# Gelu of two feature tiles in a gated attention and MLP kernel: by five instructions on two engines, or by one ScalarE activation each

## The chip, the cores and the metric

The kernel runs on one core of a Trainium2 chip. A core has five engines that each work through a queue of their own in order: TensorE (PE, matrix products into PSUM), VectorE (DVE), ScalarE (ACT, activation functions), GpSimd (POOL) and SyncE (SP, which here issues the DMA transfers). They wait for one another by semaphores. PSUM has eight banks of 128 partitions by 512 floats. The metric is the time of one execution on the device, in microseconds (us).

## The reference

Two branches are computed from one input `x` (2048 tokens by 448 features) and mixed by a gate per token:

```python
g = sigmoid((x * gate_w).sum(-1))          # one gate per token
a = A_ref(x, wq, wk, wv, wo, beta)         # 16 heads of 28, 4 segments of 512 tokens:
                                           # causal softmax attention in a segment, plus a memory
                                           # of the earlier segments with phi(t) = t+1 if t>0 else exp(t)
# B_ref: an MLP over the tokens
h = layernorm(x)
u = einsum('bsd,sf->bdf', h, w1) + b1      # 2048 tokens -> 1792 features, for each of 448 columns
u = gelu(u, approximate=True)              # 0.5 u (1 + tanh(sqrt(2/pi) (u + 0.044715 u^3)))
y = einsum('bdf,fs->bds', u, w2) + b2      # 1792 features -> 2048 tokens
return g * a + (1 - g) * y.transpose
```

All inputs and the output are bf16.

## The kernel before

**Tiling.** Tokens are cut into 16 tiles of 128 and four chunks (segments) of 512; heads into four groups of four. The 1792 features of the MLP are 14 tiles of 128, counted by `ft` from 0 to 13.

**The MLP.** `mm1(ft)` (L1025) makes one feature tile: 16 matmuls `u{ft}-0` to `u{ft}-15`, one for each token tile, accumulate 128 features by 448 columns in one PSUM bank. Then follow five instructions (L1035 to L1048):

- `gsq` on ScalarE: Square with scale sqrt(0.044715) and bias, from PSUM to `gg`;
- `gvh` on ScalarE or VectorE: half of u plus bias, from PSUM to `vh`;
- `garg` on VectorE: (gg + 1) vh;
- `gth` on ScalarE: Tanh of it;
- `gelu` on VectorE: (gg + 1) vh into `uT[ft]`, in bf16.

The bank is free when `gsq` and `gvh` have read it. `mm2(T)` (L1052) makes a token tile `y` of the second product from all 14 `uT` tiles; its first matmul waits for all of them. `fin` (L1063) adds the attention's part, and a transfer writes the tile out.

**The attention.** `scores(p, f)` (L912) makes the instructions `sc{p}_{f}`: scores of four heads into the four PSUM banks 0 to 3 at once. `exp{p}_{f}` on ScalarE (L933) reads all four (2048 elements a partition) and writes to a slot of SBUF; the next `sc` can only write once this `exp` has read. `mask` on GpSimd (L936) follows, then `pv` (L960) and, for the memory part, `mem` on TensorE (L947), and a chain on VectorE (L974 to L997). `wo` (L1008) is the output projection, `ag` (L1017) its gating.

**The projections.** `pair` (L664) makes two products together, for q, k or v of a chunk: `lo` (for example `lok3_0`) starts the accumulation of both products in two banks, each on half of the array's rows; `prk3_0` and the like finish them. `cpk`, `cpq` and `cpv` (L701, L759, L783) copy the results out of PSUM, on ScalarE (a Copy activation) or VectorE. `ek` and `eq` (L744, L768) are the Exp of phi.

**What sets the order.** Nothing is decided while the kernel runs. `ORDER` (L286) lists by name what each engine does, in order, as a planner left it. `name@banks` says which of the PSUM banks 4 to 7 (for an `exp`, which slot) the instruction takes: `lok3_0@54` accumulates its two products in banks 5 and 4. `u12-0@7*5` is `u12-0` to `u12-4`, beginning in bank 7. `Sched.plan` (L157) gives an instruction that takes a bank a dependence on everything that used the bank's last content, and `finalize` (L212) turns dependences into semaphore waits. Every matmul is issued through `mm` (L261), so most matmuls carry the line L264 in the profile.

Around the change ScalarE's order is: `exp4_1`, `gsq13`, `eq2_2`, `gvh13`, `exp4_2`, `gsq12`, `gth13`, `cpk3_0`, `exp4_3`, `cpk3_2`, `cpk3_3`, `gth12`, `exp4_4`, `ag4`, `ag5`, `exp5_0`. TensorE's is: `sc4_2`, `u12-5` to `u12-15`, `lok3_0`, `prk3_0`, `sc4_3`, `prk3_1`, `lok3_2`, `prk3_2`, `prx3_3`, `loq3_0`, `sc4_4`, `prq3_0`, `pv8`, `wo4`, `wo5`, `sc5_0`, and later `y0`. Tile 13 is made before tile 12: `u13` is in bank 6, `u12` in bank 7.

An activation function is read from a table that ScalarE has loaded; the compiler puts an `ACT_TABLE_LOAD` in front of an activation whose function the loaded table lacks. The kernel before has one, at its start.

Of the kernel before, what the change touches and what calls it, by code (L numbers as in the profile page):

```python
# [5 lines left out]
ACT = mybir.ActivationFunctionType  # L6
# [6 lines left out]
D = 448  # L13
# [61 lines left out]
class Sched:  # L75
# [13 lines left out]
    def op(self, eng, fn, reads=(), writes=(), name=None, dma=False, out=False, cost=100.0, prio=0.0, mode="f",  # L89
           nbytes=0, rel=0.0, port=False, take=None, use=(), alt=None, space=None,  # L90
           hold=HOLD):

        o = Op()
        o.eng, o.fn, o.name, o.idx = eng, fn, name, len(self.ops)
        o.is_event, o.ev_val, o.knowledge, o.waits = False, None, None, None
        o.cost = cost
        o.lat = LAT[eng]
        o.hold = hold  # L100
        o.prio = (prio, o.idx)
        o.mode = mode
        o.tile = mode if mode in "rh" else "f"
        o.cols = False
        o.nbytes = nbytes
        o.rel = rel
        o.port = port
        o.take = take if isinstance(take, list) else [take] if take is not None else []
        o.free = use
        for g in use:  # L110
            g.left += 1
        o.alts = {eng: (fn, cost, port)}
        if alt is not None:
            o.alts[alt[0]] = (alt[1], alt[2], False)
            o.eng = None
        o.start = o.end = o.pos = None
        o.evspace = eng if alt is None else None
        if dma:
            self._dma_uid += 1
            o.evspace = space or "dma_u%d" % self._dma_uid  # L120
            o.is_event = True
        if out:
            self.out_spaces.add(o.evspace)
        deps, order = {}, {}

        def need(d):
            if d is not o:
                deps[d.idx] = d

        def after(d):  # L130
            if d is not o:
                order[d.idx] = d

        for r in reads:
            if r.last_write is not None:
                need(r.last_write)
            if r.psum and eng != "PE":
                for rd in r.reads:
                    if rd.eng != "PE" and (rd.eng != o.eng or o.eng is None):
                        need(rd)  # L140
        for r in writes:
            w = r.last_write
            if w is not None:
                (after if r.psum and eng == "PE" and w.evspace == "PE" else need)(w)
            for rd in r.reads:
                (after if r.psum and eng == "PE" and rd.evspace == "PE" else need)(rd)
        o.deps = list(deps.values())
        o.order = list(order.values())
        for r in reads:
            r.reads.append(o)  # L150
        for r in writes:
            r.last_write = o
            r.reads = []
        self.ops.append(o)
        return o
# [112 lines left out]
def pe_cost(*cols):  # L268
    return sum(max(c, 64) / 2.4 + 2.0 for c in cols)


def act_cost(n, sbuf=False, ptr=0):
    return n / 1.2 + (95.0 if sbuf else 50.0) + 92.0 * ptr
# [6 lines left out]
def pool_cost(n):  # L280
    return n / 1.2 + 180.0
# [12 lines left out]
u7-11*5 loq2_0@57 prq2_0 prq2_1 u9-0@6 sc2_2 u9-1*3 loq2_2@57 prq2_2h mem4@4 u9-4*5 sc2_3 u9-9*7 prq2_2 pv4@4 sc2_4  # L294
wo1@5 wo0#1@6 wo2@4 sc3_0 wo3@7 lot8@64 prt8 prt9 mem5@7 sc3_1 pv5@7 u10-0@6*6 sc3_2 lot10@57 prt10 prt11 mem6@4
u10-6*5 sc3_3 mst1@5 u10-11*5 u11-0@4*2 pv6@5 sc3_4 u11-2*14 u13-0@6 sc4_0 u13-1*7 mem7@5 pv7@4 u13-8 sc4_1 u13-9*7
u12-0@7*5 sc4_2 u12-5*11 lok3_0@54 prk3_0 sc4_3 prk3_1 lok3_2@67 prk3_2 prx3_3 loq3_0@54 sc4_4 prq3_0 pv8@6 wo4@7
wo5@5 sc5_0 wo6@6 wo7@7 pv9@5 mem9@6 prq3_1 sc5_1 y0-0@7*13 sc5_2 y0-13 y2-0@5*4 mem8@4 y2-4*5 sc5_3 y2-9*5 mem10@6
y1-0@7*2 pv10@4 sc5_4 y1-2*11 sc6_0 y1-13 y4-0@5*10 sc6_1 y4-10*4 y5-0@7*7 sc6_2 mem11@4 pv11@5 y5-7*4 lot14@64
prt14 sc6_3 y5-11*3 y3-0@5*9 sc6_4 mst2@7 y3-9*4 loq3_2@67 prq3_2h prq3_2 y3-13 prt15 y6-0@6*2 sc7_0 lot12@57 prt12  # L300
prt13 y6-2*5 sc7_1 y6-7 pv12@4 pv13@5 wo8@7 mem12@4 y6-8*3 wo10@5 wo11@7 mem14@4 y6-11 y11-0@5*4 mem13@7 sc7_2
# [7 lines left out]
exp1_0@5 gth1 gth0 exp1_1@6 gsq2 gvh2 gsq3 gth2 gth3 gsq4 gvh4 ek1_0 gth4 ek0_3 eq1_3 exp1_2@2 gsq6 gvh6 exp1_3@3  # L309
gth6 gsq5 exp1_4@0 ek1_1 gth5 exp2_0@1 gsq8 ek1_2 gvh8 exp2_1@4 gsq7 gth8 exp2_2@5 gth7 ek1_3 exp2_3@6 gsq9 cpq2_2  # L310
exp2_4@0 gth9 ag0 ag2 exp3_0@2 cpv8 cpv9 gt8 exp3_1@3 gt9 eq2_1 ek2_0 exp3_2@1 cpv11 gt10 ek2_1 exp3_3@4 gsq10
eq2_3 gvh10 exp3_4@0 gth10 gsq11 exp4_0@5 gt11 eq2_0 gth11 exp4_1@6 gsq13 eq2_2 gvh13 exp4_2@7 gsq12 gth13 cpk3_0
exp4_3@2 cpk3_2 cpk3_3 gth12 exp4_4@3 ag4 ag5 exp5_0@0 ek2_2 eq3_0 cpq3_1 exp5_1@1 eq3_1 exp5_2@4 exp5_3@5 ek2_3
exp5_4@6 exp6_0@2 exp6_1@3 exp6_2@7 cpv14 exp6_3@0 gt14 exp6_4@1 cpq3_2 cpq3_2#1 cpv15 eq3_2 gt15 exp7_0@4 cpv12
gt12 gt13 exp7_1@5 ag8 ag10 ag11 eq3_3 exp7_2@6 exp7_3@2 exp7_4@3 ag9 ag12 ag13 ag14 ag15""",
    "DVE": """
# [7 lines left out]
msta0 mk1_1 mstc0 mstc0#1 mstc0#2 mstc0#3 gelu5 ta3 phk1_1 mk1_2 garg8 phk1_2 cpq2_0 cpq2_1 gvh7 gelu8 garg7 rec3  # L324
tm4 gelu7 oa3 eps4 mk1_3 ot3 gvh9 ta4 garg9 rec4 cpq2_2#1 oa4 gelu9 ag3 om4 phk1_3 tm5 ag1 eps5 ta5 ot4 rec5 mq2_1
cpv10 oa5 phq2_1 tm6 om5 msta1 eps6 mk2_0 mstc1 ta6 mstc1#1 mstc1#2 mstc1#3 garg10 rec6 ot5 om6 gvh11 gelu10 garg11
tm7 oa6 gelu11 eps7 ta7 phk2_0 rec7 ot6 garg13 om7 oa7 gvh12 gelu13 cpk3_1 garg12 ot7 cpq3_3 cpq3_0 gelu12 ta8
gcol2 mq2_2 omg2 mq2_3 ag6 b2g2 ag7 ta9 phq2_3 mk2_2 mk2_1 phk2_2 phk2_1 mq2_0 tm9 phq2_0 fin0 eps9 tm8 rec9 eps8
phq2_2 rec8 oa9 oa8 fin2 om9 mk2_3 om8 fin1 ot9 phk2_3 ta10 fin4 ot8 tm10 tm11 eps10 ta11 eps11 rec10 rec11 oa10
om10 fin5 oa11 msta2 ot10 mstc2 mstc2#1 mstc2#2 fin3 mstc2#3 om11 mq3_0 mq3_2 cpv13 ot11 gcol3 phq3_0 ta12 omg3  # L330
# [25 lines left out]
def build_kernel(nc, X, WQ, WK, WV, WO, BETA, W1, B1, W2, B2, GW, OUT):  # L356
    NSL, NP = 3, 5
    sch = Sched(nc, {"psum": (4, 5, 6, 7), "p": tuple(range(NP))}, {"p": (NP, NP + 1, NP + 2)})
    op = sch.op
# [10 lines left out]
    def sb(shape, dt=BF16):  # L370
        return hold(nc.sbuf_tensor(shape, dt))
# [9 lines left out]
    def bank(b):  # L381
        return ps[:, b.bank if isinstance(b, Bank) else b, :]

    def bres(b):
        return b.res if isinstance(b, Bank) else R_bank[b]
# [4 lines left out]
    def buse(b):  # L390
        return {"use": (b,)} if isinstance(b, Bank) else {}
# [17 lines left out]
    uT = sb([128, NFT, D])  # L409
# [12 lines left out]
    b1c = sb([128, NFT], F32)  # L422
# [54 lines left out]
    R_uT = R("uT", NFT)  # L477
# [6 lines left out]
    R_ident, R_bst, R_beta, R_bias, R_b2g = R("ident"), R("bst", 2), R("beta"), R("bias"), R("b2g")  # L484
# [35 lines left out]
    for st, rs, name in ((gstage, R_gst, "g"), (bstage, R_bst, "b")):  # L520
        op("POOL", lambda e, st=st: e.memset(st[:].bitcast(U32), 0), writes=rs, name="sz" + name, cost=100, prio=-5.0)
    op("SP", lambda e: e.dma_start(gstage[0:3, :], GW[0:384].rearrange("(c p) -> c p", p=128)),
       writes=[R_gst[0]], name="ldgw", dma=True, prio=-3, cost=500, nbytes=2000)
    op("SP", lambda e: e.dma_start(gstage[3:4, :], GW[320:448].rearrange("(c p) -> c p", p=128)),
       writes=[R_gst[1]], name="ldgwb", dma=True, prio=-3, cost=500, nbytes=2000)
# [5 lines left out]
       name="ldbeta", dma=True, prio=-3, cost=500, nbytes=8000)  # L531
    op("SP", lambda e: e.dma_start(bstage[0:NFT, :], B1.rearrange("(t p) -> t p", p=128)), writes=[R_bst[0]],
       name="ldb1", dma=True, prio=-3, cost=500, nbytes=8000)
    op("SP", lambda e: e.dma_start(bstage[NFT : NFT + NT, :], B2.rearrange("(t p) -> t p", p=128)),
       writes=[R_bst[1]], name="ldb2", dma=True, prio=-3, cost=500, nbytes=8000)
# [5 lines left out]
    def ring_load():  # L541
# [15 lines left out]
    P_BASE, P_ATT, P_PROJ, P_WO, P_M1, P_M2 = 0.0, 100.0, 200.0, 300.0, 400.0, 500.0  # L557
# [9 lines left out]
       reads=[R_ident], writes=[R_ident], name="id1", cost=300)  # L567
# [8 lines left out]
    for k, ap in enumerate((kT[:, 3, :], qT[:, 3, :])):  # L576
        op("POOL", lambda e, ap=ap: e.memset(ap.bitcast(U32), 0), writes=[R_z3[k]] + (R_qT if k else R_kT)[3],
           name=f"z3_{k}", cost=pool_cost(S // 2))
    vpad = vaug.bitcast(U32).rearrange("p t (h c) -> p (t h) c", c=16)
    for k, val in enumerate((0x3F80, 0)):  # L580
        op("POOL", lambda e, k=k, val=val: e.memset(vpad[:, :, 14 + k : 15 + k], val), reads=R_v if k else [], writes=R_v,
           name=f"v{k}", cost=pool_cost(256))
# [442 lines left out]
    def mm1(ft):  # L1025
        b = Bank()
        q = ft % 2
        fb, f2 = divmod(ft, 2)
        w1c = slots[fb % NSL].rearrange("p (t f) -> p t f", t=NT)
        for st in range(NT):  # L1030
            op("PE", lambda e, cols=False, st=st: mm(e, bank(b)[:, 0:D], w1c[:, st, f2 * 128 : f2 * 128 + 128],
                                                     xh[:, st, :], cols, start=(st == 0), stop=(st == NT - 1)),
               reads=[R_slot[fb % NSL][st // 4], R_x[st]], writes=[bres(b)], take=b if st == 0 else None, name=f"u{ft}-{st}", mode="x", cost=pe_cost(448),
               prio=P_M1 + ft)
        op("ACT", lambda e: e.activation(gg[:, q, :], bank(b)[:, 0:D], ACT.Square, bias=b1s[:, ft : ft + 1],  # L1035
                                         scale=math.sqrt(GC)),
           **buse(b), reads=[bres(b), R_bias], writes=[R_gg[q]], name=f"gsq{ft}", cost=act_cost(448, ptr=1), prio=P_BASE)
        op("ACT", lambda e: e.activation(vh[:, q, :], bank(b)[:, 0:D], ACT.Identity, bias=b1h[:, ft : ft + 1],  # L1038
                                         scale=0.5),
           **buse(b), reads=[bres(b), R_bias], writes=[R_vh[q]], name=f"gvh{ft}", cost=act_cost(448, ptr=1), prio=P_BASE,  # L1040
           alt=("DVE", lambda e: e.tensor_scalar(vh[:, q, :], bank(b)[:, 0:D], 0.5, b1h[:, ft : ft + 1], op0=ALU.mult,  # L1041
                                                 op1=ALU.add), dve_cost(448)))
        op("DVE", lambda e: e.scalar_tensor_tensor(gg[:, q, :], gg[:, q, :], 1.0, vh[:, q, :], op0=ALU.add,  # L1043
                                                   op1=ALU.mult),
           reads=[R_gg[q], R_vh[q]], writes=[R_gg[q]], name=f"garg{ft}", cost=535, port=True, prio=P_BASE)
        op("ACT", lambda e: e.activation(gg[:, q, :], gg[:, q, :], ACT.Tanh, scale=2.0 * GS), reads=[R_gg[q]],  # L1046
           writes=[R_gg[q]], name=f"gth{ft}", cost=act_cost(448, True), prio=P_BASE)
        op("DVE", lambda e: e.scalar_tensor_tensor(uT[:, ft, :], gg[:, q, :], 1.0, vh[:, q, :], op0=ALU.add,  # L1048
                                                   op1=ALU.mult),
           reads=[R_gg[q], R_vh[q]], writes=[R_uT[ft]], name=f"gelu{ft}", cost=535, port=True, prio=P_BASE)  # L1050
# [143 lines left out]
```

## Time and profile before

| | |
|---|---|
| median of 3 runs | 176.94 us (176.91 to 177.38) |
| profiled execution, span from first to last instruction | 175.3 us |
| between that span and the median (what lies around it) | 1.64 us |
| TensorE (PE) busy | 169.6 us |
| VectorE (DVE) busy | 149.3 us |
| ScalarE (ACT) busy | 133.7 us |
| GpSimd (POOL) busy | 69.3 us |
| mean granted TensorE clock | 1.000 |

The page gives the span as the profiled execution's own time; the times of the runs are measured from outside it. A busy time counts the instructions of an engine from start to end, merged where they overlap. Matmuls are pipelined and their ends are modelled, so a busy TensorE is not the same as TensorE at its peak. The chain of waits follows the work that ended last back from the end: at each step to what released it. "Idle before, releaser" is the time an engine stood still ahead of an instruction, and whose semaphore ended it.

### The profile page before, as it was taken

Reading aid. Unit: us, or ns where it says so; the run is one execution under the profiler, and the core shown is the slowest. Engines: PE = TensorE matmul, PEld = TensorE weight load, DVE = VectorE, ACT = ScalarE, POOL = GpSimd, SP = SyncE. Lnnn points to the kernel's source line nnn. Section 1 sums busy time; section 2 is a strip of 40 time slices with the busy share of each in tenths; the row PEclk is TensorE's granted clock in tenths of the full one; section 3 lists DMA queues with packets and bytes.
Section 4 is the critical chain, followed back from the end, with each engine's and each line's share of the span. In section 5 each row is a group of like instructions: output and inputs, shape, how many; then the busy total and the mean of one; then the engine's idle time right before and its main releaser. Section 6 shows DMA issues by size and latency. Waiting matters only on the chain.

```text
span 175.3 us, 5601 instructions
## 1 busy us (share of the span) xinstructions
PE 169.6 (97%) x2354; PEld 82.0 (47%) x2354; DVE 149.3 (85%) x337; ACT 133.7 (76%) x170; POOL 69.3 (40%) x93
## 2 busy tenths in 40 slices
PE   8899999899999999998999999999999999999994
PEld 3443434345544544534544344444444544555653
DVE  5599999799995899998999999997889999893213
ACT  2377898999589999999999999987878977404200
POOL 8002027442302234346846644359474435550000
PEclk9999999999999999999999999999999999999999
DMA  5989973799939726942061440208567100366221
GB/s 145 295 155 290 265 148 86 176 303 228 218 105 251 210 62 184 240 105 49 0 173 41 120 130 24 60 26 243 135 193 207 51 2 4 111 184 196 69 82 52
DMA packets 50472, 24.62 MB, mean 140 GB/s; under 512 B 14976, under 2 KB 50208, under 8 KB 50448
## 3 DMA queue, kind: packets, MB, share of 16 engines
q1 hardware_dynamic: 50160, 24.05, 56.0%
q8 instruction: 18, 0.29, 0.8%
q10 hardware_dynamic: 288, 0.23, 0.4%
q14 instruction: 6, 0.05, 0.1%
HBM read 18.76 MB, written 2.36 MB: 121 GB/s over the span
## 4 chain that ended last, share of the span: by engine, by line
PE 89%; DVE 5%; DMA 3%; ACT 1%; SPq 0%; issue 0%
PE t L264 76%; PE t L924 7%; PE t L960 5%; DMA t<-in_A_wk_dram 3%; PE t L810 1%; DVE t L1048 1%; DVE t L987 0%; DVE t L883 0%; ACT t L701 0%; DVE t L703 0%; DVE t L1041 0%; ACT t L1035 0%; DVE t L1021 0%; DVE t L974 0%; DVE t L976 0%
## 5 line engine op out<-in xcount | busy, mean ns | idle before, releaser
L264 PE MATMUL t<-t 128*32 128x448 bf16 (+10 forms) x1620 | 145.3, 346 | 1.9 <-DVE t L619 0.7
L264 PEld LDWEIGHTS t<-t 128*32 128x32 bf16 (+2 forms) x1620 | 66.5, 97 | 67.1 <-issue 13.3
L933 ACT ACTIVATE t<-t 128x2048 bf16<-128x2048 f32 x40 | 75.7, 1892 | 6.0 <-PE t L924 5.8
L936 POOL TENSOR_SCALAR_AFFINE_SELECT t<-t 128x512 bf16<-128x512 bf16 x64 | 46.9, 734 | 57.6 <-ACT t L933 53.8
L1063 DVE SCALAR_TENSOR_TENSOR t<-t 128x448 bf16<-128x448 f32 (+2 forms) x17 | 10.9, 652 | 12.8 <-PE t L264 12.8
L991 POOL TENSOR_TENSOR t<-t 128x448 bf16<-128x448 f32 x12 | 14.6, 1217 | 9.7 <-DVE t L989 9.1
L1017 ACT ACTIVATE t<-t 128x448 bf16<-128x448 f32 x12 | 8.5, 726 | 10.3 <-PE t L264 10.1
L924 PE MATMUL t<-t 28*128 28x512 bf16 (+3 forms) x256 | 15.8, 301 | 0.0
L876 POOL TENSOR_TENSOR t<-t 128x4 f32<-128x4 f32 x4 | 4.5, 1130 | 20.3 <-DVE t L874 20.3
L960 PE MATMUL t<-t 128*32 128x512 bf16 (+3 forms) x256 | 11.3, 299 | 0.6 <-DVE t L974 0.6
L976 DVE STREAM_TRANSPOSE t<-t 128x512 f32<-128x512 f32 x16 | 11.2, 700 | 0.8 <-PE t L960 0.8
L924 PEld LDWEIGHTS t<-t 28*128 28x128 bf16 x256 | 4.5, 92 | 13.8 <-ACT t L933 7.4
L997 DVE STREAM_TRANSPOSE t<-t 128x512 bf16<-128x512 bf16 x16 | 10.9, 687 | 0.0
L1043 DVE SCALAR_TENSOR_TENSOR t<-t 128x448 f32<-128x448 f32 x14 | 8.8, 636 | 1.5 <-ACT t L1038 1.5
L1048 DVE SCALAR_TENSOR_TENSOR t<-t 128x448 bf16<-128x448 f32 x14 | 9.8, 705 | 0.2 <-ACT t L1046 0.2
L1035 ACT ACTIVATE t<-t 128x448 f32<-128x448 f32 x14 | 9.1, 656 | 1.1 <-PE t L264 1.1
L867 DVE BATCH_NORM_STATS2 t<-t 128x6 f32<-128x448 bf16 x16 | 9.4, 607 | 0.1
L1046 ACT ACTIVATE t<-t 128x448 f32<-128x448 f32 x14 | 8.2, 598 | 1.5 <-DVE t L1043 1.5
L960 PEld LDWEIGHTS t<-t 128*32 128x32 bf16 x256 | 6.8, 97 | 5.4 <-DVE t L974 0.8
L987 DVE SCALAR_TENSOR_TENSOR t<-t 128x448 f32<-128x448 f32 x12 | 9.2, 775 | 0.1
L974 DVE STREAM_TRANSPOSE t<-t 128x512 f32<-128x512 f32 x12 | 8.4, 697 | 0.4
L989 DVE TENSOR_TENSOR t<-t 128x448 f32<-128x448 f32 x12 | 8.2, 685 | 0.0
(69 smaller groups left out, 143.5 us busy)
## 6 DMA issues: line engine op xcount, KB each, us to landing
t<-in_B_w_dram SPq DMA_DIRECT2D x52, 256.0 KB, 4.1
out_dram<-t SPq DMA_DIRECT2D x15, 112.0 KB, 1.8
t<-in_A_x_dram SPq DMA_DIRECT2D x3, 448.0 KB, 4.6
t<-in_B_w_dram SPq DMA_DIRECT2D x8, 128.0 KB, 3.8
t<-in_A_wo_dram SPq DMA_DIRECT2D x4, 98.0 KB
t<-in_A_wq_dram SPq DMA_DIRECT2D x1, 336.0 KB, 5.3
t<-in_A_wv_dram SPq DMA_DIRECT2D x1, 336.0 KB, 5.5
spare_heads<-t SPq DMA_DIRECT2D x8, 32.0 KB
```

The source lines that it names most:

```text
L264: last = e.matmul(out[q], w[:, q], x, skip_group_check=True, **kw)
L867: op("DVE", lambda e: e.bn_stats(st6[:, t, :], xh[:, t, :]), reads=[R_x[t]], writes=[R_st6[t]], name=f"bns{t}", cost=512, prio=P_PROJ - 10 ...
L924: last = e.matmul(bank(hl)[:, c0 : c0 + w], kT[r, hg, s * 512 + j * 128 : s * 512 + j * 128 + 128], qT[r, hg, s * 512 + 128 * j : s * 512 ...
L933: op("ACT", lambda e: e.activation(pslot(g), ps[:, 0:4, :], ACT.Exp, scale=SCALE), reads=R_bank[0:4], writes=[g.res], take=g, name=f"exp{p ...
L936: op("POOL", lambda e, c0=c0: e.affine_select(pslot(g)[:, :, c0 : c0 + 128], pslot(g)[:, :, c0 : c0 + 128], pattern=[[0, 4], [1, 128]], co ...
L960: last = e.matmul(bank(cb)[32 * hl : 32 * hl + 32, 128 * j : 512], vaug[:, 4 * s + j, 32 * h : 32 * h + 32], pslot(P_fill[u // 2][f])[:, h ...
L976: dv(lambda e: e.transpose(t2[:, 0, :], bank(cb)[:, 0:512]), [bres(cb)], [R_tt[tb][0]], "ta", 630, use=(cb,))
L987: dv(lambda e: e.scalar_tensor_tensor(n3[0], n3[0], oc, rb[0], op0=ALU.mult, op1=ALU.mult), [R_tt[tb][0], R_rec[tb], R_omcol], [R_tt[tb][0 ...
L991: op("POOL", lambda e: e.tensor_tensor(o3, n3[0], n3[1], op=ALU.add), reads=R_tt[tb], writes=[R_ob[tb]], name=f"o{u}", cost=1280, port=Tru ...
L997: dv(lambda e: e.transpose(oT[:, hg, s * 512 : s * 512 + 512], o), [R_ob[tb]], qres(hg, s), "ot", 635)
L1048: op("DVE", lambda e: e.scalar_tensor_tensor(uT[:, ft, :], gg[:, q, :], 1.0, vh[:, q, :], op0=ALU.add, op1=ALU.mult), reads=[R_gg[q], R_vh ...
L1063: op("DVE", lambda e: e.scalar_tensor_tensor(outst[:, p, c0:c1], bank(b)[:, 0 : c1 - c0], omg[:, T : T + 1], ag(T)[:, c0:c1], op0=ALU.mult ...
```

## The change

For tiles 12 and 13 the five instructions are replaced by one activation, `gl12` and `gl13`: ScalarE's own Gelu function in its tanh form, read from PSUM with the bias column `b1c`, written to `uT` in bf16. Its table is not the one that Exp is read from, so the table is switched ahead of them and again before the next function that it lacks. The other twelve tiles stay as they were. In `ORDER` the instructions that are gone are taken out; `gl13` and `gl12` stand one after the other between `exp4_2` and `cpk3_0`; and the banks of three later pairs and two output projections are renumbered.

```diff
 "PE"
 u12-0@7*5 sc4_2 ...
-                    u12-5*11 lok3_0@54 prk3_0 sc4_3 prk3_1 lok3_2@67 prk3_2 prx3_3 loq3_0@54 sc4_4 prq3_0 pv8@6 wo4@7
-wo5@5 sc5_0 wo6@6 wo7@7 ...
+                    u12-5*11 lok3_0@74 prk3_0 sc4_3 prk3_1 lok3_2@65 prk3_2 prx3_3 loq3_0@74 sc4_4 prq3_0 pv8@6 wo4@5
+wo5@7 sc5_0 wo6@6 wo7@7 ...
 "ACT"
-... exp4_1@6 gsq13 eq2_2 gvh13 exp4_2@7 gsq12 gth13 cpk3_0
-exp4_3@2 cpk3_2 cpk3_3 gth12 exp4_4@3 ag4 ag5 ...
+... exp4_1@6 eq2_2 exp4_2@7 gl13 gl12 cpk3_0
+exp4_3@2 cpk3_2 cpk3_3 exp4_4@3 ag4 ag5 ...
 "DVE"
-tm7 oa6 gelu11 eps7 ta7 phk2_0 rec7 ot6 garg13 om7 oa7 gvh12 gelu13 cpk3_1 garg12 ot7 cpq3_3 cpq3_0 gelu12 ta8
+tm7 oa6 gelu11 eps7 ta7 phk2_0 rec7 ot6 om7 oa7 cpk3_1 ot7 cpq3_3 cpq3_0 ta8
 def mm1(ft): ... # after the 16 matmuls
+        if ft >= 12:
+            op("ACT", lambda e: e.activation(uT[:, ft, :], bank(b)[:, 0:D], ACT.Gelu_apprx_tanh,
+                                             bias=b1c[:, ft : ft + 1], scale=1.0),
+               **buse(b), reads=[bres(b), R_bias], writes=[R_uT[ft]], name=f"gl{ft}", cost=act_cost(448, ptr=1), prio=P_BASE)
+            return
```

More of the change, by code (lines that the diff above doesn't have):

```diff
@@ L296 @@
 u10-6*5 sc3_3 mst1@5 u10-11*5 u11-0@4*2 pv6@5 sc3_4 u11-2*14 u13-0@6 sc4_0 u13-1*7 mem7@5 pv7@4 u13-8 sc4_1 u13-9*7
-u12-0@7*5 sc4_2 u12-5*11 lok3_0@54 prk3_0 sc4_3 prk3_1 lok3_2@67 prk3_2 prx3_3 loq3_0@54 sc4_4 prq3_0 pv8@6 wo4@7
-wo5@5 sc5_0 wo6@6 wo7@7 pv9@5 mem9@6 prq3_1 sc5_1 y0-0@7*13 sc5_2 y0-13 y2-0@5*4 mem8@4 y2-4*5 sc5_3 y2-9*5 mem10@6
+u12-0@7*5 sc4_2 u12-5*11 lok3_0@74 prk3_0 sc4_3 prk3_1 lok3_2@65 prk3_2 prx3_3 loq3_0@74 sc4_4 prq3_0 pv8@6 wo4@5
+wo5@7 sc5_0 wo6@6 wo7@7 pv9@5 mem9@6 prq3_1 sc5_1 y0-0@7*13 sc5_2 y0-13 y2-0@5*4 mem8@4 y2-4*5 sc5_3 y2-9*5 mem10@6
 y1-0@7*2 pv10@4 sc5_4 y1-2*11 sc6_0 y1-13 y4-0@5*10 sc6_1 y4-10*4 y5-0@7*7 sc6_2 mem11@4 pv11@5 y5-7*4 lot14@64
@@ L311 @@
 exp2_4@0 gth9 ag0 ag2 exp3_0@2 cpv8 cpv9 gt8 exp3_1@3 gt9 eq2_1 ek2_0 exp3_2@1 cpv11 gt10 ek2_1 exp3_3@4 gsq10
-eq2_3 gvh10 exp3_4@0 gth10 gsq11 exp4_0@5 gt11 eq2_0 gth11 exp4_1@6 gsq13 eq2_2 gvh13 exp4_2@7 gsq12 gth13 cpk3_0
-exp4_3@2 cpk3_2 cpk3_3 gth12 exp4_4@3 ag4 ag5 exp5_0@0 ek2_2 eq3_0 cpq3_1 exp5_1@1 eq3_1 exp5_2@4 exp5_3@5 ek2_3
+eq2_3 gvh10 exp3_4@0 gth10 gsq11 exp4_0@5 gt11 eq2_0 gth11 exp4_1@6 eq2_2 exp4_2@7 gl13 gl12 cpk3_0
+exp4_3@2 cpk3_2 cpk3_3 exp4_4@3 ag4 ag5 exp5_0@0 ek2_2 eq3_0 cpq3_1 exp5_1@1 eq3_1 exp5_2@4 exp5_3@5 ek2_3
 exp5_4@6 exp6_0@2 exp6_1@3 exp6_2@7 cpv14 exp6_3@0 gt14 exp6_4@1 cpq3_2 cpq3_2#1 cpv15 eq3_2 gt15 exp7_0@4 cpv12
```

## The prediction

> **What bounds the kernel now.** First the busy times and the chain of waits on the page of the kernel before: which engine sets the end?
>
> ```profile
> PE 169.6 (97%) x2354; PEld 82.0 (47%) x2354; DVE 149.3 (85%) x337; ACT 133.7 (76%) x170; POOL 69.3 (40%) x93
> ...
> PE 89%; DVE 5%; DMA 3%; ACT 1%; SPq 0%; issue 0%
> ```
>
> TensorE is busy 97% of the span and is 89% of the chain that ended last. An average can hide stages, so next the busy times by stretch, cut where the change lies (us; columns PE, PEld, DVE, ACT, POOL, each with its instructions, then granted clock, DMA share, GB/s).
>
> ```profile
> 95.84:99.43 3.59, 3.59 (x28) 1.42 (x28) 3.41 (x8) 3.59 (x6) 1.87 (x3) 1.00 0.19 40
> 99.43:102.56 3.13, 3.13 (x21) 1.01 (x25) 3.13 (x5) 3.13 (x5) 2.78 (x4) 1.00 0.98 276
> ...
> 111.96:152.80 40.84, 40.84 (x623) 19.88 (x627) 37.74 (x75) 31.29 (x30) 23.65 (x29) 1.00 0.39 106
> ```
>
> TensorE has no idle time from here to 152.80. Where tiles 12 and 13 get their Gelu (95 to 103 us), ScalarE is just as full, and so nearly is VectorE. Later ScalarE has slack (31.29 of 40.84). So three engines run level at the change, and behind it TensorE alone sets the pace. A full bar of TensorE is modelled, so I checked it against the chain in order of time (start, length, what):
>
> ```profile
> 78.76 0.64 DVE t L974
> ...
> 93.46 2.38 PE t L264 x12
> 95.84 0.33 PE t L924 x8
> 96.17 3.26 PE t L264 x16
> 99.43 0.33 PE t L924 x4
> 99.76 2.80 PE t L264 x13
> 102.56 0.33 PE t L924 x8
> ...
> 105.70 0.33 PE t L924 x4
> ...
> 111.96 0.33 PE t L924 x8
> 112.29 2.21 PE t L264 x11
> ...
> 117.36 2.19 PE t L264 x11
> ...
> 119.87 2.19 PE t L264 x11
> ...
> 122.39 2.19 PE t L264 x11
> ...
> 172.94 0.35 DVE t L1063
> ```
>
> Eleven matmuls of the second MLP product take 2.19 us each time, twelve of the first 2.38: 0.19 us a matmul and some 0.1 for changing the array's tiling. Pieces that equal to 0.02 us are a pace, not waits. By the kernel's order the pieces around the change are: 95.84 scores sc4_2; 96.17 the last eleven matmuls of u12 (2.19, so to 98.36), then lok3_0 and prk3_0 (1.07, to 99.43); 99.43 sc4_3; 99.76 the other third-chunk projections (2.80); 102.56 sc4_4; 105.70 sc5_0.
>
> **The change part by part.** ScalarE in the same stretch, one line an instruction (start, length):
>
> ```profile
> 93.61 1.93 ACT L933 ACTIVATE t<-t 128x2048 bf16<-128x2048 f32 x1
> 95.36 0.69 ACT L1035 ACTIVATE t<-t 128x448 f32<-128x448 f32 x1
> 95.88 0.69 ACT L768 ACTIVATE t<-t 128x512 bf16<-128x512 bf16 x1
> 96.40 0.70 ACT L1038 ACTIVATE t<-t 128x448 f32<-128x448 f32 x1
> 96.92 1.95 ACT L933 ACTIVATE t<-t 128x2048 bf16<-128x2048 f32 x1
> 98.67 0.72 ACT L1035 ACTIVATE t<-t 128x448 f32<-128x448 f32 x1
> 99.19 0.67 ACT L1046 ACTIVATE t<-t 128x448 f32<-128x448 f32 x1
> 99.66 0.69 ACT L701 ACTIVATE t<-t 128x512 bf16<-128x512 f32 x1
> 100.13 1.98 ACT L933 ACTIVATE t<-t 128x2048 bf16<-128x2048 f32 x1
> ...
> 102.84 0.60 ACT L1046 ACTIVATE t<-t 128x448 f32<-128x448 f32 x1
> 103.31 1.89 ACT L933 ACTIVATE t<-t 128x2048 bf16<-128x2048 f32 x1
> ...
> 112.34 1.88 ACT L933 ACTIVATE t<-t 128x2048 bf16<-128x2048 f32 x1 [0.28 <-PE t L924]
> ```
>
> These are exp4_1, gsq13, eq2_2, gvh13, exp4_2, gsq12, gth13, cpk3_0, exp4_3, gth12, exp4_4 and, as one that waited for TensorE, exp5_2. An activation starts before the last one ends: small ones come 0.47 to 0.52 us apart, and 1.75 us lie between the start of an exp and the next start.
>
> *Removed from ScalarE:* gsq13, gvh13, gsq12 (0.52 each by starts), gth13 and gth12 (0.47 each): 2.50 us. *Removed from VectorE:* garg and gelu twice, gvh12 once. Their rows, with those of the only table load:
>
> ```profile
> L1043 DVE SCALAR_TENSOR_TENSOR t<-t 128x448 f32<-128x448 f32 x14 | 8.8, 636 | 1.5 <-ACT t L1038 1.5
> L1048 DVE SCALAR_TENSOR_TENSOR t<-t 128x448 bf16<-128x448 f32 x14 | 9.8, 705 | 0.2 <-ACT t L1046 0.2
> L1041 DVE TENSOR_SCALAR t<-t 128x448 f32<-128x448 f32 x8 | 5.3, 679 | 0.6 <-ACT t L1035 0.4
> ```
>
> ```profile
> 1.71 1.28 ACT L661 ACT_TABLE_LOAD   x1 [1.71 <-PEq L1179]
> 4.86 0.60 ACT L661 ACTIVATE t<-t 128x512 bf16<-128x512 bf16 x1 [1.87 <-PE t L645]
> ```
>
> ```profile
> L1035 ACT ACTIVATE t<-t 128x448 f32<-128x448 f32 x14 | 9.1, 656 | 1.1 <-PE t L264 1.1
> ```
>
> VectorE sheds 2 x 0.636 + 2 x 0.705 + 0.679 = 3.36 us. I count it at no gain: the chain has no VectorE piece between those at 78.76 and 172.94 us; TensorE's own work covers it.
>
> *Added:* gl13 and gl12. No Gelu is in the trace; it has the shape, the PSUM input and the one bias column of the Square on L1035, so 0.656 us, starts 0.52 apart. And two table switches, Exp's table to Gelu's ahead of gl13 and back ahead of exp4_3. The one load shown takes 1.28 us; the next activation came 1.87 us after it, waiting for TensorE. So a switch costs between nothing (if it ran beside other work) and 1.28 + 1.87 = 3.15 us (if all of that idle time belonged to it). I take 1.28, from the end of one activation to the start of the next, because the 1.87 is put down to the transpose on L645. ScalarE thus gets 1.04 + 2.56 us for 2.50.
>
> Here a rule speaks against the change: the Trainium skill, "ScalarE: Activation LUTs", section "What ACT_TABLE_LOAD costs", adds a drain of about 1.38 us to each load, 2.66 us a switch; the sum below would be 5.8 in place of 3.1 us. "ScalarE activation tables: per-element evaluation and per-set limits", section "What a function is on this engine", has two sets one load of 1283 ns apart, which is the row's figure; no row here shows a drain.
>
> *Moved:* bank 7 is where u12 accumulates, and lok3_0, which took banks 5 and 4, now takes 7 and 4. A bank passes on when its readers are done, so TensorE's in-order queue now stands at lok3_0 until gl12 has ended; behind it stand prk3_0, sc4_3 and all else. lok3_2 gets bank 6 (gl13) and 5: free by then. The queues of SP and POOL keep their order; their transfers and masks move along with their producers. Removing garg, gelu and gvh12 moves VectorE's casts up, which nothing waits for.
>
> **The sum**, in the profiled execution's own times:
>
> 1. exp4_2 no longer stands behind gvh13. It starts as exp5_2 did, 0.05 us after its scores (111.96 + 0.33 = 112.29 against 112.34): 96.17 + 0.05 = 96.22, ending at 98.10.
> 2. Load to 99.38. gl13 from there, gl12 from 99.90 to 100.56.
> 3. lok3_0 at 100.61 in place of 98.36: **first stall, 2.25 us**.
> 4. prk3_0 ends 1.07 later, 101.68; sc4_3 ends at 102.01; the projections would end at 104.81.
> 5. cpk3_0 (ScalarE, a Copy, waiting for prk3_0) runs 101.73 to 102.42, the second load to 103.70, exp4_3 to 105.58.
> 6. sc4_4 needs the four score banks that exp4_3 reads: 105.63 in place of 104.81: **second stall, 0.82 us**. Against 102.56 before, all is 3.07 us late.
>
> Is more late, or is it won back? exp4_4 starts once exp4_3, cpk3_2 and cpk3_3 are issued (103.70 + 1.75 + 0.47 + 0.47 = 106.39) and ends at 108.28; sc5_0 comes up at 105.63 + 3.14 = 108.77 (102.56 to 105.70 before). It clears it by 0.49, as before (103.31 + 1.89 = 105.20 against 105.70). Then TensorE works with nothing idle to 152.80, so it cannot win anything back. Span 175.3 + 3.07 = 178.4; the median of the runs, 176.94, lies 1.64 above the span, so the time is 176.94 + 3.07 = **180.0 us**.
>
> **The rivals.**
>
> *A. A switch costs more than the load.* The pipeline drains before it, or refills after it. With the bound of 3.15: gl12 ends at 102.43, stall 4.12; exp4_3 ends at 109.32, sc4_4 at 109.37, 6.8 us late: 183.7. Any part of it counts twice, so half the extra gives 181.9. For it: nothing ran straight after the load shown. Against: that idle time has a cause of its own.
>
> By the Trainium skill's 2.66 us ("ScalarE: Activation LUTs", "What ACT_TABLE_LOAD costs") the same steps end 5.8 us late, an estimate of 182.8. No run here shows it yet.
>
> *B. The second load stands ahead of cpk3_0.* Then it runs 100.56 to 101.84 while TensorE does lok3_0 and prk3_0; exp4_3 starts at 102.31 and ends at 104.19, before TensorE is ready at 104.81. Only the first stall stays: 2.25, 179.2. For it: a pass could reload at once. Against: one load serves the Copies, Exps, Tanhs and Squares of the whole kernel before, so a table seems to hold such simple functions, and the Copy needs no switch.
>
> *C. The loads cost no time* (run beside an exp, or not needed). gl13 starts at 97.97, gl12 ends at 99.15, lok3_0 at 99.20: 0.84 late, and sc4_4 does not wait: 177.8. For it: the first load hid behind other waits. Against: exp4_2 uses the table that the load replaces.
>
> *D. Not slower: TensorE's modelled records hide waits for VectorE.* VectorE is busy 3.13 of 3.13 us at the change; were it the true pace of the stretch to 152.80, its 3.36 us less would meet the 3.07 us of stalls: 176.94 + 3.07 - 3.36 = 176.6. It decides once the records hide 3 us of such waits. Against: equal pieces of 2.19 us, and no VectorE piece in the chain there.
>
> **How the numbers follow.** Forecast (179.5 to 180.6) 0.62; A 0.15; B 0.08; C 0.09; D 0.06. The range 178.9 to 182.9 holds the forecast, B and most of A; it leaves out C, D and A's far end, nearly 0.2. This measurement tells 0.3% (0.53 us) from no change; the three runs shown spread as little. C is slower by more than that; D is mostly within it: faster 0.02, same 0.04, slower 0.94.
>
> **What would show it.** Two table loads near 98 and 102 us, 1.28 us long, the second behind a Copy; exp4_2 starting near 96.2; a gap on TensorE of about 2.2 us released by the line of the Gelu, and one of 0.8 released by L933; the pieces after that unchanged, 3.1 us later; VectorE some 3.4 us less busy and no faster for it. No gap ahead of lok3_0, gaps over 3 us, or shorter pieces after 106 us would make the prediction wrong.

## The result, and the profile after

The changed kernel takes 181.52 us (median of four runs, 180.95 to 181.70) against 177.06 us for the kernel before beside it. The ratio taken over all the runs is 1.0243, 95% interval 1.0218 to 1.0268 (the two medians alone give 1.0252). It is slower by 2.4%, some 4.3 us. The profiled execution spans 179.6 us against 175.3, also 4.3 us more. The forecast was 180.0, within 178.9 to 182.9.

The page of the changed kernel, busy times and the chain that ended last by engine:

```profile
PE 170.5 (95%) x2346; PEld 82.1 (46%) x2354; DVE 146.0 (81%) x332; ACT 135.4 (75%) x169; POOL 68.8 (38%) x93
...
PE 81%; DVE 8%; ACT 5%; DMA 3%; issue 1%; SPq 0%
```

VectorE sheds 3.3 us, ScalarE gains 1.7, and ScalarE's share of the chain goes from 1% to 5%. Where, its timeline shows (start, length, then the idle time and what ended it):

```profile
95.39 0.67 ACT L768 ACTIVATE t<-t 128x512 bf16<-128x512 bf16 x1
96.25 1.88 ACT L933 ACTIVATE t<-t 128x2048 bf16<-128x2048 f32 x1 [0.18 <-PE t L924]
98.14 1.28 ACT L1036 ACT_TABLE_LOAD   x1
99.44 1.16 ACT L1036 ACTIVATE t<-t 128x448 bf16<-128x448 f32 x2
102.78 0.60 ACT L701 ACTIVATE t<-t 128x512 bf16<-128x512 f32 x1 [2.18 <-PE t L264]
103.40 1.28 ACT L933 ACT_TABLE_LOAD   x1
104.69 1.88 ACT L933 ACTIVATE t<-t 128x2048 bf16<-128x2048 f32 x1
```

These are eq2_2, exp4_2, the first load, both Gelu activations, cpk3_0, the second load and exp4_3. Each load takes 1.28 us and fills the gap between its neighbours but for 0.01 to 0.02 us. The second stands behind the Copy. TensorE's timeline of the same stretch:

```profile
95.80 0.40 PE L924 MATMUL t<-t 28*128 28x256 bf16 x8
96.13 2.25 PE L264 MATMUL t<-t 128*128 128x448 bf16 x11
100.74 0.61 PE L264 MATMUL t<-t 64*128 64x512 bf16 x2 [2.36 <-ACT t L1036]
101.69 1.06 PE L264 MATMUL t<-t 128*128 128x512 bf16 x2 [0.33 <-issue]
102.68 0.61 PE L924 MATMUL t<-t 28*128 28x512 bf16 x4
103.22 3.24 PE L264 MATMUL t<-t 128*128 128x512 bf16 x13
106.62 0.40 PE L924 MATMUL t<-t 28*128 28x384 bf16 x8 [0.16 <-ACT t L933]
...
109.94 0.40 PE L924 MATMUL t<-t 28*128 28x512 bf16 x4
```

They are sc4_2, the rest of u12, lok3_0, prk3_0, sc4_3, the projections, sc4_4 and sc5_0. lok3_0 waits 2.36 us for the Gelu. But then lok3_0 and prk3_0 take 1.94 us until sc4_3 (1.07 before), and the projections 3.24 in place of 2.87 (the timeline before follows below). The granted clock fits that (busy times in short windows; the third number from the end is the clock):

```profile
100.40:100.60 0.20, 0.00 (x0) 0.00 (x0) 0.00 (x0) 0.20 (x1) 0.20 (x1) 1.00 1.14 336
100.60:100.80 0.20, 0.06 (x2) 0.09 (x2) 0.00 (x0) 0.00 (x0) 0.20 (x1) 0.51 1.14 340
...
103.80:104.00 0.20, 0.20 (x2) 0.00 (x0) 0.00 (x0) 0.20 (x1) 0.00 (x0) 0.50 0.00 0
104.00:104.20 0.20, 0.20 (x2) 0.00 (x0) 0.00 (x0) 0.20 (x1) 0.00 (x0) 0.95 0.00 0
```

After 2.2 us of idle time the clock fell to half, and stayed there for 3.4 us, to 104.0.

Executions differ by some tenths in their first microseconds (the first weight load took 4.42 us in the execution of before, up to 5.13 in others), so from here on I compare the distance from sc4_2 to sc5_0, the stretch in which the change acts. The timeline of TensorE before, sc4_2, sc4_3, the projections and sc5_0:

```profile
95.77 0.40 PE L924 MATMUL t<-t 28*128 28x256 bf16 x8
...
99.36 0.39 PE L924 MATMUL t<-t 28*128 28x512 bf16 x4
99.69 2.87 PE L264 MATMUL t<-t 128*128 128x512 bf16 x13
...
105.64 0.39 PE L924 MATMUL t<-t 28*128 28x512 bf16 x4
```

9.87 us before; 95.80 to 109.94 = 14.14 after: 4.27 us more, the whole difference of the spans.

### The profile page after: what moved, and what is told of

Its sections match the earlier page's. It is cut to its first block, busy times and chain, and to the rows that moved or that the text cites. A ratio compares the mean times of both kernels' runs of the same rounds, so it can differ in the third digit from the quotient of the medians.

```text
span 179.6 us, 5586 instructions
## 1 busy us (share of the span) xinstructions
PE 170.5 (95%) x2346; PEld 82.1 (46%) x2354; DVE 146.0 (81%) x332; ACT 135.4 (75%) x169; POOL 68.8 (38%) x93
## 3 DMA queue, kind: packets, MB, share of 16 engines
HBM read 18.76 MB, written 2.36 MB: 118 GB/s over the span
## 4 chain that ended last, share of the span: by engine, by line
PE 81%; DVE 8%; ACT 5%; DMA 3%; issue 1%; SPq 0%
PE t L264 69%; PE t L924 6%; PE t L960 4%; DMA t<-in_A_wk_dram 3%; ACT t L933 2%; DVE t L1021 1%; DVE t L748 1%; PE t L810 1%; ACT t L701 1%; ACT L933 1%; ACT L1036 1%; DVE t L773 1%; DVE t L974 1%; DVE t L976 1%; ACT t L1036 1%
## 5 line engine op out<-in xcount | busy, mean ns | idle before, releaser
L264 PE MATMUL t<-t 128*32 128x448 bf16 (+9 forms) x1612 | 145.5, 347 | 5.0 <-ACT t L1036 2.4
L987 DVE SCALAR_TENSOR_TENSOR t<-t 128x448 f32<-128x448 f32 x12 | 9.2, 774 | 0.1
L701 ACT ACTIVATE t<-t 128x512 bf16<-128x512 f32 (+1 forms) x12 | 6.0, 508 | 4.2 <-PE t L264 4.1
L1048 DVE SCALAR_TENSOR_TENSOR t<-t 128x448 f32<-128x448 f32 x12 | 7.6, 642 | 1.5 <-ACT t L1043 1.5
L748 DVE SCALAR_TENSOR_TENSOR t<-t 128x512 bf16<-128x512 bf16 x12 | 8.4, 707 | 0.0
L1051 ACT ACTIVATE t<-t 128x448 f32<-128x448 f32 x12 | 6.9, 582 | 1.8 <-DVE t L1048 1.8
```

Source lines behind the costliest of these rows:

```text
L264: last = e.matmul(out[q], w[:, q], x, skip_group_check=True, **kw)
L748: op("DVE", lambda e: e.scalar_tensor_tensor(kphi[:, p, :], ks, 0.0, kphi[:, p, :], op0=ALU.max, op1=ALU.add), reads=kres(hg, tc) + [R_kph ...
```

## The experiments

The theory after the result: three things on TensorE, in a row. It waits at lok3_0 for bank 7, that is for the Gelu behind the first load; its clock falls; and sc4_4 waits for exp4_3, which stands behind the second load. VectorE's relief gives nothing. Rivals: the loads cost the time whatever the banks; the clock is only a label; VectorE was the hidden pace.

### The banks of before

```diff
-u12-5*11 lok3_0@74 ... lok3_2@65 ... loq3_0@74 ... wo4@5 wo5@7
+u12-5*11 lok3_0@54 ... lok3_2@67 ... loq3_0@54 ... wo4@7 wo5@5
```

> The changed kernel with only the PSUM bank numbers of the kernel before (lok3_0 in 5 and 4 again, lok3_2 in 6 and 7, loq3_0 in 5 and 4, wo4 in 7, wo5 in 5). Theory: the 4.4 us are TensorE standing still at lok3_0 for bank 7 (2.37 us), then running at half the granted clock until 104 us, then waiting for exp4_3 behind the second table load. With the banks back lok3_0 runs at 98.4 without a wait; lok3_2 waits 0.3 us for gl12; sc4_4 waits for exp4_3, which ends near 104.3, so it comes 1.8 us later than before in place of 4.06; no single stall over 1.6 us, so the clock stays at 1.0: 178.9 us. Rival (the two table loads and their time on ScalarE set the loss, whatever the banks): as after, 181.5 us.

Measured: 178.90 us against 176.94 before, ratio 1.0120 (1.0095 to 1.0145). TensorE's timeline, sc4_2, sc4_4 and sc5_0:

```profile
95.60 0.40 PE L924 MATMUL t<-t 28*128 28x256 bf16 x8
...
104.13 0.40 PE L924 MATMUL t<-t 28*128 28x384 bf16 x8 [1.56 <-ACT t L933]
...
107.44 0.39 PE L924 MATMUL t<-t 28*128 28x512 bf16 x4
```

11.84 us, 1.97 more than before, and the stall is now the one for exp4_3 alone. So with the banks of before the loads cost 2 us. The renumbering of the banks is the rest of the change's loss in its profiled execution: 2.30 of 4.27 us, the fallen clock included. With the clock held, as further down, it is 1.44 of 3.41.

### No switch of the table

```diff
-e.activation(uT[:, ft, :], bank(b)[:, 0:D], ACT.Gelu_apprx_tanh,
+e.activation(uT[:, ft, :], bank(b)[:, 0:D], ACT.Tanh,
```

> The changed kernel, banks as changed, but gl12 and gl13 apply Tanh, which the loaded table serves, in place of Gelu: no table is switched, and the output is not the reference's. Theory: gl12 ends near 99.15, lok3_0 waits 0.85 us for it, nothing else waits and the clock stays at 1.0: 177.9 us. Rival (the bank order alone costs the time, the loads hardly matter): over 179.5 us.

Measured: 178.33 against 176.94, ratio 1.0078 (1.0059 to 1.0098). sc4_2, lok3_0 and sc5_0:

```profile
96.12 0.40 PE L924 MATMUL t<-t 28*128 28x256 bf16 x8
...
99.63 0.39 PE L264 MATMUL t<-t 64*128 64x512 bf16 x2 [0.93 <-ACT t L1036]
...
106.99 0.39 PE L924 MATMUL t<-t 28*128 28x512 bf16 x4
```

10.87 us, 1.00 more than before. This is what the bank costs by itself with the new order of ScalarE; 0.85 was expected. The median is 0.4 us further up than this stretch explains. In the profiled execution sc4_2 comes 0.35 us later than before (96.12 against 95.77), so that much lies ahead of the stretch; of the other executions no trace shows it.

### Both undone

```diff
-ACT.Gelu_apprx_tanh ... lok3_0@74 ... lok3_2@65 ... loq3_0@74 ... wo4@5 wo5@7
+ACT.Tanh            ... lok3_0@54 ... lok3_2@67 ... loq3_0@54 ... wo4@7 wo5@5
```

> The changed kernel without its two hurts: Tanh in place of Gelu in gl12 and gl13 (no table switch, the output is not the reference's) and the bank numbers of before. What is left of the change is 3.36 us less on VectorE and 1.46 us less on ScalarE. Theory: TensorE had no idle time to give, so the work taken away buys nothing: 177.0 us, within 0.3 us of before. Rival D of the prediction (VectorE was the hidden pace): 174 to 176 us.

Measured: 177.31 against 177.21, ratio 0.9997 (0.9971 to 1.0023). sc4_2 and sc5_0:

```profile
96.27 0.40 PE L924 MATMUL t<-t 28*128 28x256 bf16 x8
...
106.14 0.39 PE L924 MATMUL t<-t 28*128 28x512 bf16 x4
```

9.87 us, to the hundredth what it was. VectorE's and ScalarE's relief is worth nothing here, and rival D falls.

### The banks alone, in the kernel before

```diff
 # the kernel before, with its five instructions for every tile
-u12-5*11 lok3_0@54 ... lok3_2@67 ... loq3_0@54 ... wo4@7 wo5@5
+u12-5*11 lok3_0@74 ... lok3_2@65 ... loq3_0@74 ... wo4@5 wo5@7
```

> The kernel before with only the changed bank numbers: lok3_0 takes bank 7, which gsq12 and gvh12 read. No Gelu activation, no table load. Theory: lok3_0 waits for gvh12 on VectorE, which ends at 100.1, so a stall of 1.8 us; exp4_3 ends near 103.7, before TensorE is at sc4_4: 1.8 us later than before, 178.9 us if the clock stays at 1.0, about 1 us more if it falls after a stall of that length. Rival (the new banks are harmless by themselves): 177.1 us.

Measured: 179.22 against 176.94, ratio 1.0134 (1.0119 to 1.0149). sc4_2, lok3_0 and sc5_0:

```profile
96.02 0.40 PE L924 MATMUL t<-t 28*128 28x256 bf16 x8
...
100.50 0.39 PE L264 MATMUL t<-t 64*128 64x512 bf16 x2 [1.89 <-DVE t L1041]
...
107.85 0.39 PE L924 MATMUL t<-t 28*128 28x512 bf16 x4
```

11.83 us, 1.96 more: the renumbered banks alone cost as much as two table loads. After 1.89 us of idle time the mean clock was still 1.0, in each of the four executions.

### Work in the stall, to hold the clock

```diff
-u12-5*11 lok3_0@74 prk3_0 ...
+u12-5*11 fill@5 lok3_0@74 prk3_0 ...   # 9 matmuls of 128x512 into bank 5, read by nobody
```

> The changed kernel with nine matmuls of 128x512 that nobody reads put ahead of lok3_0, in bank 5, which is free then: 1.95 us of work where TensorE stood still for 2.37 us. Theory: they start at 98.36 and end near 100.3, lok3_0 still starts when gl12 has ended, near 100.7; but the granted clock stays at 1.0, so lok3_0 to sc4_4 take their old time, exp4_3 ends near 105.6 and sc4_4 comes 3.1 us later than before, as the sum of the prediction has it: 180.1 us, 1.4 us faster than without the added work. Rival (the clock is only a label of the idle time, or the loss after the stall has another cause): 181.5 us.

Measured: 180.81 against 176.94, ratio 1.0219 (1.0204 to 1.0234). sc4_2, lok3_0, sc4_4 and sc5_0:

```profile
96.08 0.40 PE L924 MATMUL t<-t 28*128 28x256 bf16 x8
...
101.02 1.15 PE L264 MATMUL t<-t 64*128 64x512 bf16 x5 [0.39 <-ACT t L1036]
...
106.04 0.40 PE L924 MATMUL t<-t 28*128 28x384 bf16 x8 [0.75 <-ACT t L933]
...
109.36 0.39 PE L924 MATMUL t<-t 28*128 28x512 bf16 x4
```

lok3_0 comes 4.94 us after sc4_2, as in the changed kernel (100.74 - 95.80): the added work delays nothing. The pieces behind it have their old length (lok3_0 and prk3_0 1.08 us until sc4_3), sc4_4 waits 0.75 us for exp4_3, and the whole is 13.28 us, 3.41 more than before. Against the 4.27 of the changed kernel the fallen clock is worth 0.86 us in its profiled execution. By the medians it is less, and there the intervals overlap: 180.81 lies halfway between the theory's 180.1 and the rival's 181.5. So the held clock is shown by the trace, and its worth in the time only roughly.

### The second load moved up

One Exp of a single column after gl12 makes the second load run there:

```diff
-gl13 gl12 cpk3_0
+gl13 gl12 xx cpk3_0     # xx: Exp of one column of b1c into a spare tile
```

> The kernel with the nine added matmuls (clock kept at 1.0) and besides an Exp of one column after gl12, so that the second table load runs at once, ahead of cpk3_0, while TensorE does lok3_0 and prk3_0. Theory: the second stall (0.75 us at sc4_4 with the added matmuls alone) goes, and with it the 0.16 us by which wo4 then waits for the copies behind exp4_3; only the stall at lok3_0 stays, 2.4 us: 179.4 us. Rival (where the load stands makes no difference): 180.8 us.

> The changed kernel with only the Exp of one column after gl12, no added matmuls. Theory: at half the clock TensorE reaches sc4_4 only 0.16 us before exp4_3 ends, so the slow clock has swallowed the second stall, and moving the load up wins only those 0.16 us and the 0.16 us at wo4: 181.1 us. Rival (the second load's place is worth the 0.82 us of the prediction here too): 180.6 us.

Measured: with the added matmuls 179.68 against 177.21, ratio 1.0130 (1.0084 to 1.0176); without them 180.05, ratio 1.0157 (1.0105 to 1.0208), its runs from 179.27 to 181.11. The first two lines are sc4_2 and sc5_0 with the added matmuls; then, without them, sc4_2, lok3_0, sc4_3, sc4_4 and sc5_0:

```profile
95.28 0.40 PE L924 MATMUL t<-t 28*128 28x256 bf16 x8
...
107.58 0.39 PE L924 MATMUL t<-t 28*128 28x512 bf16 x4
```

```profile
95.62 0.40 PE L924 MATMUL t<-t 28*128 28x256 bf16 x8
...
100.56 0.39 PE L264 MATMUL t<-t 64*128 64x512 bf16 x2 [2.36 <-ACT t L1036]
...
101.64 0.40 PE L924 MATMUL t<-t 28*128 28x512 bf16 x4
...
104.77 0.40 PE L924 MATMUL t<-t 28*128 28x384 bf16 x8
...
107.92 0.39 PE L924 MATMUL t<-t 28*128 28x512 bf16 x4
```

12.30 us in both, 2.43 more than before: the second stall is gone and only the one at lok3_0 is left. The first kernel came out as the theory said. The second did not come out as written: it supposed a slow clock, but in this execution the clock stayed at 1.0 after the very 2.36 us of idle time after which it had fallen. That makes it a control for the clock, with no work added: from lok3_0 to sc4_3 it takes 1.08 us, where the changed kernel took 1.94. Of its four executions two had a mean clock of 1.0 (179.27 and 179.57 us) and two of 0.99 (181.11 and 180.53), which is what 3.4 us at half speed would give. No trace shows the latter two, and the kernel with the added matmuls, at 1.0 in all four, itself spreads by 1.4 us; so what the earlier load is worth under a slow clock stays open.

### How often the clock falls

The changed kernel once more, and beside it one with four added matmuls in place of nine:

```diff
-        for _ in range(9):
+        for _ in range(4):
             last = e.matmul(bank(fb_), ones[:, 0:128], ones, start=True, stop=True, ...)
```

> The changed kernel once more, beside the next kernel on one chip, to see how often the clock falls. With the Exp moved up, the same 2.36 us of idle time ahead of lok3_0 left the clock at 1.0 in the profiled execution, and that kernel's times lie 1.8 us apart. Theory: the clock falls in some executions and not in others after the same idle time; the times of this kernel spread over more than 1 us, with a median near 181.3 us. Rival (in this kernel the clock falls each time): a spread as in the kernel before and a median of 181.5 us.

> The changed kernel with four unread matmuls of 128x512 ahead of lok3_0 in place of nine: TensorE works 0.87 us more after u12 and then idles 1.5 us in place of 2.4. Theory: idle times of 0.9 us and 1.9 us left the clock at 1.0, so this does too; the stall at lok3_0 and the wait at sc4_4 (0.75 us) stay: 180.4 us, with a small spread, and 0.5 to 1 us under the changed kernel beside it. Rival (it is the work in the stall's last part that counts): as the changed kernel, 181.4 us.

Measured: 181.10 against 177.09, ratio 1.0235 (1.0180 to 1.0290), five of six times between 180.81 and 181.33; with four matmuls 180.91, ratio 1.0203 (1.0160 to 1.0246). The changed kernel, its lok3_0 and sc4_4, then the clock where it fell and where it came back:

```profile
100.52 1.57 PE L264 MATMUL t<-t 64*128 64x512 bf16 x5 [2.36 <-ACT t L1036]
...
106.22 0.40 PE L924 MATMUL t<-t 28*128 28x384 bf16 x8
```

```profile
101.00:101.20 0.20, 0.20 (x2) 0.11 (x1) 0.00 (x0) 0.00 (x0) 0.00 (x0) 0.77 0.98 292
...
104.40:104.60 0.20, 0.20 (x3) 0.11 (x2) 0.20 (x1) 0.20 (x1) 0.00 (x0) 0.70 0.00 0
```

It fell again, but 0.6 us after lok3_0 had begun, for 3.4 us once more; sc4_2 to sc5_0 took 13.79 us (95.58 to 109.37), 3.92 more than before. With four matmuls, lok3_0, sc4_4 and sc5_0:

```profile
100.88 1.15 PE L264 MATMUL t<-t 64*128 64x512 bf16 x5 [1.49 <-ACT t L1036]
...
105.91 0.40 PE L924 MATMUL t<-t 28*128 28x384 bf16 x8 [0.75 <-ACT t L933]
...
109.22 0.39 PE L924 MATMUL t<-t 28*128 28x512 bf16 x4
```

From sc4_2 at 95.94 that is 13.28 us again, with the clock at 1.0: idle time of 1.5 us left it alone, and the mean clock was 0.999 or 1.0 in all six executions. But its median is 0.2 us under the changed kernel's, where 0.5 to 1 us was expected, and its times spread by 1.2 us; by the times alone the two can't be told apart.

On the clock the theory holds. The mean clock of the changed kernel's executions is 0.99 in four of these six and in three of the first four, and 1.0 in the others; so the same idle time lowers the clock in some executions and not in others. On the times it does not hold: the spread of more than 1 us hangs on a single time (182.97), and the two executions at 1.0 (180.81 and 181.05) are not clear of those at 0.99 (180.87 and up). Why the same idle time does the one or the other is not settled by these runs.

### The order of TensorE fitted to the late exp

```diff
-lok3_0@74 prk3_0 sc4_3 prk3_1 lok3_2@65 prk3_2 prx3_3 loq3_0@74 sc4_4 prq3_0 pv8@6 wo4@5 wo5@7 sc5_0 wo6@6 wo7@7
+lok3_0@54 prk3_0 sc4_3 prk3_1 lok3_2@67 prk3_2 prx3_3 loq3_0@54 prq3_0 pv8@6 sc4_4 wo4@7 wo5@5 wo6@6 sc5_0 wo7@7
 # cpk3_2 and cpk3_3 from ScalarE to VectorE
```

> The changed kernel with the real Gelu and both switches, the bank numbers of before, and TensorE's order changed so that it has work while exp4_3 is late: sc4_4 moves behind prq3_0 and pv8, sc5_0 behind wo6; cpk3_2 and cpk3_3 move from ScalarE to VectorE, which has the room, so that their banks come free. Theory: TensorE's idle time is the whole loss, so what remains is 0.3 us at lok3_2 and some tenths at sc4_4 and sc5_2: 177.6 us. Rival (ScalarE's longer work comes back as a late exp further on, all the same): as with the banks alone, 178.9 us. Neither has it faster than before.

Measured: 178.29 against 177.21, ratio 1.0056 (1.0031 to 1.0080). The scores sc4_2, sc4_4 and sc5_2:

```profile
96.06 0.40 PE L924 MATMUL t<-t 28*128 28x256 bf16 x8
...
104.58 0.40 PE L924 MATMUL t<-t 28*128 28x384 bf16 x8 [0.26 <-ACT t L933]
...
113.26 0.40 PE L924 MATMUL t<-t 28*128 28x256 bf16 x8 [0.33 <-ACT t L933]
```

With the Gelu, both loads and the same scheme the loss is 1.0 us in place of 4.3. The time lies between the 177.6 us that the theory gave and the rival's 178.9: part of the late exp came back at sc5_2, as the rival had it, though not all. This is the best form of the change that was run, and it is still slower than the kernel before; the experiments point to none that beats it.

## Why the prediction was right, and where it was not

*Right: the chain of steps.* Step 1: exp4_2 starts 0.02 us after its scores end, at 96.25 (96.22). Step 2: load from 98.14, Gelu from 99.44 to 100.60 (98.10, 99.38, 100.56). Step 3: the stall is 2.36 us (2.25). The switch costs its load and nothing else, and the second load stands behind the Copy. The gain of VectorE is nothing, shown by undoing the two changes that cost time, the loads and the banks. Nothing is won back: sc5_1 is 4.3 us late (113.30 against 109.00), and so is the end.

On the price of a switch the Trainium skill's two pages differ. The measurement decides for "ScalarE activation tables: per-element evaluation and per-set limits", section "What a function is on this engine" (one load of 1283 ns): 1.31 us lie between exp4_2's end and the first Gelu, not the 2.66 us that "ScalarE: Activation LUTs", section "What ACT_TABLE_LOAD costs", gives with its drain.

*Wrong: step 4, "prk3_0 ends 1.07 later".* It took 1.94 us from lok3_0 to sc4_3, since the clock fell to half. I had read the clock at 1.0 everywhere and never asked what 2.25 us of idle time would do to it. It is the largest term missed: 0.86 us of the stretch in this execution, 0.51 (13.79 against 13.28) in the second. The slow work itself is longer: lok3_0 to sc4_4 took 4.21 us with the load moved up and the clock at 1.0, but 5.72 without its wait here and 5.70 in the second execution, some 1.5 us more. Part of that fell into time in which TensorE would have waited for exp4_3 anyway. So the slow clock also changed step 6: TensorE reached sc4_4 so late that it waited 0.16 us there in place of 0.82. With the clock held, that wait was 0.75: the step was right under the condition that I had assumed.

*Wrong: "sc5_0 comes up at 105.63 + 3.14".* It came 3.32 us after sc4_4 (106.62 to 109.94). VectorE's timeline after the change:

```profile
107.56 0.69 DVE L714 CAST t<-t 64x512 bf16<-64x512 f32 x1 [1.79 <-ACT t L712]
```

The bank of prx3_3 is read by two copies, cpk3_3 on ScalarE and cpq3_3 on VectorE; the kernel lets the second wait for the first (L137 to L140), and the first stands behind the late exp4_3. wo4 needs the bank from both. I had followed exp4_3 to exp4_4, but not to the copies behind it, and had said of VectorE's casts that nothing waits for them; this one cost 0.17 us.

The sum by the runs: 3.07 forecast; 0.17 more until lok3_0 starts (2.42 us later than before, if its start before is counted back 1.07 us from sc4_3; 2.25 was forecast, with 0.05 us between gl12's end and lok3_0, where the trace shows 0.14); 0.17 at wo4; together 3.41, what the kernel with the clock held shows; 0.86 for the clock; 4.27. The mechanism and sign were right, and the measured time lies in the range; but it lies above the forecast's own 179.5 to 180.6, and the range reached that far only for the sake of rival A, whose dearer switch the traces do not show. That the range held is luck: the clock, which the sum put at nothing without a reason, filled the room left for another cause. B and C fell too: the second load waited for the Copy, and both loads cost their full time.

## What to carry to other kernels

Ask of an instruction that replaces five where its result is awaited, not what it saves: here the engines that were relieved had no say in the time, and the two loads stood between two exps that TensorE counted on. When a queue in order is to wait some microseconds, look at what is behind it and at the clock, not only at the wait. And a bank number is a dependence: giving the next user the bank that is freed last can cost the whole wait for it (a gap of 0.93 us cost 1.00, one of 1.89 cost 1.96).

## What the runs showed that I had not expected

TensorE's granted clock fell to 0.5 after 2.2 us of idle time in one execution, 0.6 us after the work had begun again in another, and not at all in a third, all three with the same 2.36 us gap; each time that it fell it stayed down for 3.4 us. By the mean clocks it fell in nine of the fourteen executions of the two kernels with that gap. Gaps of 0.93, 1.49, 1.56 and 1.89 us left it at 0.999 or 1.0 in all eighteen executions of their kernels. The Trainium skill, "TensorE: Matmul & The Clock Gate", section "Part 1: The HAM clock gate (the "warmup" mystery)", has the clock fall to half after an idle window of about 3.4 us, with windows that run freely. The half agrees with the traces, and 3.4 us is the time for which the clock stayed down; that the array must stand idle for 3.4 us does not agree, since the gap was 2.36. That a window which is mostly idle is enough, depending on where the gap lies in it, would fit all three executions, but is argued and not shown.
